# Linear attention in front of a hardswish MLP: softmax sums of five batches in 32-row column tiles, their reciprocals spread by DMA through DRAM

**Chip, cores, metric.** One core of one Trainium2 chip. The time is device microseconds of one execution of the whole program; medians of repeated runs. A difference of 2% (10.2 us here) counts as faster or slower.

## The reference, cut to what matters

```python
k_proj = einsum('ks,bhsd->bhkd', E, k)          # 8 batches, 8 heads, 1024 tokens, 64 wide -> 64 keys
v_proj = einsum('ks,bhsd->bhkd', F, v)
attn = exp(q @ k_proj.T / 8 - max)
attn = attn / (attn.sum(-1) + 1e-9)             # the softmax sums
x = (attn @ v_proj), heads side by side         # 8192 x 512
h = x @ w_in                                    # 512 -> 2048
out = (h * clip(h + 3, 0, 6) / 6) @ w_out       # 2048 -> 512
```

## The kernel before

The MLP of batch b runs as 32 "w_in groups" (4 matmuls of 128x128x512 each) and 8 "w_out groups" (16 such matmuls). The attention of batch b+1 is slipped between them at four places ("visits", n = 0 to 3, one for each w_out group). PSUM is two pools of four buffers of 128x512: `mm` and `at`.

```python
def quads(self, stationary, j, allocs):           # j: a pair of heads
    tiles = [alloc() for alloc in allocs]
    for t in range(NB):                           # two halves of the tokens
        for a in range(2):                        # two heads
            r, c = t * KP, a * D
            nc.tensor.matmul(tiles[t][c:c + D]..., stationary(r, 2 * j + a),
                             self.aT[j][r:r + KP, :, a, :], start=True, stop=True)

def sums(self, j, *allocs):                       # 64x64 tiles: each sum is made 64 times, one row for each of the 64 rows it divides
    return self.quads(lambda r, h: ones[r:r + KP, :D], j, allocs)

def visit(self, n, following, later):
    ...
    if n == 1:
        den, av = self.sums(0, pmm, pmm), self.values(0, pat, pat)
        last = self.scores(3, pat)
        recs = self.inverses(den)                 # ScalarE: Ln, then Exp(-x), 512 columns each
        self.exps(3, last)
        return lambda: self.scaled(0, av, recs)   # VectorE: values times reciprocal
    ...                                           # n = 2 and 3 alike, for j = 1, 2, 3; n = 3 also projects the next batch's k and v
```

Because the sums come out 64-fold, they stand in the rows in which the values stand, and VectorE can multiply the two tiles directly. The price is TensorE: 16 matmuls a batch for 16 distinct rows of numbers.

The softmax here doesn't subtract the row's maximum and nothing guards it: scores larger than these inputs give would overflow.

## Time and profile before

| | before |
|---|---|
| median of 6 runs | 509.23 us (509.08 to 509.76) |
| span of the profiled run | 507.8 us |
| TensorE busy | 500.3 us, 99% |
| ScalarE / VectorE busy | 274.0 / 258.2 us |
| distance of two batches, steady part | 60.62 us |

Busy time over span says who bounds. At 99% of TensorE, an instruction of another engine matters only if TensorE waits for it. The lines are shown in the prediction.

### The profile page before, as it was taken

To read this page: it belongs to the slowest core of one execution; us is meant where nothing else is said; L and a number is where in the kernel's file an instruction comes from. 1 tells how busy PE (TensorE), PEld (TensorE's weight loads), DVE (VectorE), ACT (ScalarE), POOL (GpSimd) and SP (SyncE) were. 2 spreads that over 40 slices of the span, in tenths; PEclk is the share of its full clock that TensorE was granted. 3 is DMA by queue.
4 is the path that set the end of the run, shared out by engine and by line. 5 is a ranking of instruction groups with operands and counts; after the bars stand their busy time and mean duration, and the time that the engine had idled before them with its cause. 6 is when DMAs were issued, how large, how long until landed. Compare 5 with 4: busy or idle time off the path is not lost.

```text
span 507.8 us, 7202 instructions
## 1 busy us (share of the span) xinstructions
PE 500.3 (99%) x2819; PEld 226.0 (45%) x2819; DVE 258.2 (51%) x401; ACT 274.0 (54%) x493; POOL 38.0 (7%) x57
## 2 busy tenths in 40 slices
PE   7999999999999999999999999999999999999997
PEld 3444444444444444444444444444444444444444
DVE  3572736855755733565444743467444563334420
ACT  2656476567576545664466644674447654444431
POOL 8610020010010200002000020000000000000000
PEclk9999999999999999999999999999999999999999
DMA  9999999599299593516923189411110011101112
GB/s 170 200 205 207 199 154 239 100 159 172 95 174 197 96 219 72 125 42 94 224 68 84 52 139 182 104 54 32 43 41 27 36 43 42 43 21 43 41 43 83
DMA packets 74210, 55.39 MB, mean 109 GB/s; under 512 B 35520, under 2 KB 65984, under 8 KB 74176
## 3 DMA queue, kind: packets, MB, share of 16 engines
q0 software_dynamic: 31952, 29.36, 37.1%
q1 hardware_dynamic: 42000, 25.17, 19.2%
q8 instruction: 22, 0.36, 0.3%
q10 hardware_dynamic: 224, 0.39, 0.3%
q14 instruction: 12, 0.10, 0.1%
HBM read 59.24 MB, written 16.78 MB: 150 GB/s over the span
## 4 chain that ended last, share of the span: by engine, by line
PE 96%; DMA 1%; POOL 1%; ACT 0%; issue 0%; DVE 0%; ACTq 0%; POOLq 0%
PE mm L429 44%; PE mm L462 43%; PE at L181 3%; PE mm L227 2%; DMA k<-in_k_dram 1%; PE at L227 1%; PE at L209 1%; PE mm L454 1%; PE at L349 0%; PE mm L209 0%; PE at L317 0%; POOL q L97 0%; PE at L329 0%; PE mm L349 0%; POOL k L101 0%
## 5 line engine op out<-in xcount | busy, mean ns | idle before, releaser
L435 DVE SCALAR_TENSOR_TENSOR g<-r,mm 128x512 bf16<-128x512 f32 x256 | 174.2, 687 | 135.1 <-ACT r L434 133.6
L462 PE MATMUL mm<-w_out_sb,g 128*128 128x512 bf16 x1008 | 230.9, 379 | 0.0
L429 PE MATMUL mm<-xT,w_in_sb 128*128 128x512 bf16 x1024 | 230.7, 379 | 0.0
L434 ACT ACTIVATE r<-mm 128x512 f32<-128x512 f32 x256 | 152.7, 599 | 77.2 <-PE mm L429 74.4
L429 PEld LDWEIGHTS <-w_in_sb 128*128 128x128 bf16 x1024 | 99.5, 98 | 122.1 <-issue 3.8
L462 PEld LDWEIGHTS <-g 128*128 128x128 bf16 x1008 | 96.6, 98 | 119.7 <-issue 7.0
L467 ACT COPY o_sb<-mm 128x512 f32<-128x512 f32 x35 | 20.3, 587 | 91.5 <-PE mm L462 91.5
L467 DVE COPY o_sb<-mm 128x512 f32<-128x512 f32 x28 | 19.4, 692 | 67.2 <-PE mm L462 67.2
L159 ACT ACTIVATE rec<-mm 128x512 f32<-128x512 f32 x39 | 21.7, 595 | 35.7 <-PE mm L227 20.1
L163 ACT ACTIVATE rec<-rec 128x512 f32<-128x512 f32 x60 | 35.6, 638 | 0.0
L246 DVE TENSOR_TENSOR xT<-at,rec 128x512 bf16<-128x512 f32 x42 | 26.9, 683 | 4.9 <-ACT rec L163 4.3
L218 ACT ACTIVATE aT<-at 128x512 bf16<-128x512 f32 x42 | 22.1, 617 | 0.0
L199 POOL COPY mark<-kT 1x1 bf16<-1x1 bf16 x5 | 0.9, 177 | 209.1 <-DMA kT<-kp 209.1
L159 ACT ACTIVATE rec<-at 128x512 f32<-128x512 f32 x25 | 14.7, 599 | 2.3 <-PE at L349 2.3
L181 PE MATMUL at<-k,e_t 128*64 128x512 bf16 x56 | 13.4, 382 | 0.0
L181 PE MATMUL at<-v,f_t 128*64 128x512 bf16 x56 | 13.4, 382 | 0.0
L218 ACT ACTIVATE aT<-mm 128x512 bf16<-128x512 f32 x14 | 7.6, 594 | 9.5 <-PE mm L209 9.5
L190 DVE CAST vp<-at 64x512 bf16<-64x512 f32 x14 | 9.7, 694 | 0.4
L187 DVE CAST kp<-at 64x512 bf16<-64x512 f32 x14 | 8.9, 674 | 1.1 <-PE at L181 1.1
L246 DVE TENSOR_TENSOR xT<-mm,rec 128x512 bf16<-128x512 f32 x14 | 9.0, 682 | 0.8 <-PE mm L227 0.8
L181 PEld LDWEIGHTS <-e_t 128*64 128x64 bf16 x56 | 5.6, 109 | 7.2 <-PE mm L227 2.1
L227 PE MATMUL mm<-aT,ones 64*64 64x512 bf16 x70 | 8.6, 400 | 0.0
(64 smaller groups left out, 147.0 us busy)
## 6 DMA issues: line engine op xcount, KB each, us to landing
out_dram<-o_sb SPq DMA_DIRECT2D x63, 256.0 KB, 2.0
k<-in_k_dram POOLq DMA_DIRECT2D x7, 1024.0 KB, 15.8
v<-in_v_dram POOLq DMA_DIRECT2D x7, 1024.0 KB, 20.7
q<-in_q_dram POOLq DMA_DIRECT2D x7, 1024.0 KB, 10.8
w_out_sb<-in_moe_w_out_dram POOLq DMA_DIRECT2D x4, 512.0 KB, 17.1
k<-in_k_dram POOLq DMA_DIRECT2D x4, 256.0 KB, 6.5
v<-in_v_dram POOLq DMA_DIRECT2D x4, 256.0 KB, 8.2
w_in_sb<-in_moe_w_in_dram POOLq DMA_DIRECT2D x2, 512.0 KB, 10.9
```

The lines of the kernel that those rows point to most:

```text
L159: nc.scalar.activation(ln, den, AF.Ln)
L163: nc.scalar.activation(ln, ln, AF.Exp, scale=-1.0)
L181: nc.tensor.matmul(ps[e * KP:(e + 1) * KP], ef_t[e][:, so, :], kqv[self.b]["kv"[e]][:, :, so, :], start=(so == 0), stop=(so == SO - 1))
L190: nc.vector.tensor_copy(self.vp[a * KP:(a + 1) * KP], self.ps[KP:].rearrange("p (h d) -> p h d", d=D))
L218: nc.scalar.activation(self.aT[j][:, r].rearrange("p a n -> p (a n)"), tiles[r], AF.Exp, scale=scale)
L227: nc.tensor.matmul(tiles[t][c:c + D].rearrange("p (r n) -> p r n", r=2), stationary(r, 2 * j + a), self.aT[j][r:r + KP, :, a, :], start=Tr ...
L246: nc.vector.tensor_mul(self.xT[:, j, t, :], av[t], recs[t])
L429: nc.tensor.matmul(h_ps, w_in_sb[:, ko, fo * P:(fo + 1) * P], xT[:, ko, t, :], start=(ko == 0), stop=(ko == KO - 1))
L434: nc.scalar.activation(r, h_ps, AF.Relu, bias=0.5, scale=1.0 / 6.0)
L435: nc.vector.scalar_tensor_tensor(g[:, fo, :], r, 1.0, h_ps, op0=ALU.min, op1=ALU.mult)
L462: nc.tensor.matmul(o_ps, g[:, fo, c * P:(c + 1) * P], w_out_sb[:, fo, :], start=(fo == 0), stop=(fo == FO - 1))
L467: (copy or nc.scalar.copy)(o_sb, o_ps)
```

## The change

Its intent: make each softmax sum 16 times and not 64 times, with four heads beside each other in four column tiles of 32 rows (16 rows for each half of the tokens). Since the sums then stand in other rows than the values, one of 16 rows of each goes to DRAM after Ln and Exp, and comes back broadcast over 64 rows. As that takes time, the first products (VectorE) come three w_out groups after the sums. Batches 0 to 2 keep the old way. The diff is cut to what matters: an `@@` line names each part, and `...` stands for lines or pieces left out.

```diff
+    halves = consts.tile([P, NB, KP // 4], bf16, name="halves")     # ones for the half of the rows that column t sums
...
+        def all_sums(self, alloc):
+            tiles = [alloc() for _ in range(2)]
+            for h in range(H):
+                j, a, c = h // 2, h % 2, h % 4
+                nc.tensor.matmul(tiles[h // 4][32 * c:32 * c + 32].rearrange("p (r n) -> p r n", r=2),
+                                 halves.rearrange("p t i -> p (t i)"), self.aT[j][:, :, a, :],
+                                 start=True, stop=True)
...
+        def spread(self, den):
+            few = att.tile([P, 2, TOK], f32, tag="few", name="few", bufs=1)
+            inverse(few, den)
+            rows = dram.tile([H, NB, TOK], f32, tag="rows", name="rows")
+            nc.sync.dma_start(out=rows.rearrange("(k c) t n -> (c t) k n", k=2), in_=few[::16])
+            self.recs = [rec_tile() for _ in range(KO)]
+            for h in range(H):
+                nc.sync.dma_start(out=self.recs[h // 2][h % 2 * D:(h % 2 + 1) * D]...,
+                                  in_=rows[h:h + 1]....to_broadcast([D, NB * TOK]))
...
@@ inverse: one Exp over both reciprocals (1024 columns), everywhere
+        for i, d in enumerate(den):
+            log(rec, i, d)
+        nc.scalar.activation(flat, flat, AF.Exp, scale=-1.0)
@@ visits of batches 3 to 7, by w_out group n = 0 .. 7 of the batch before
+                if (b, n) == (2, 0):
+                    return lambda: second.some_scores((2, 0, 1), six), nothing
+                if (b, n) == (2, 1):
+                    return lambda: second.some_scores((3,), six[1:2]), nothing
+                if (b, n) == (2, 3):
+                    return nothing, lambda: third.projected(pmm)
+                if n == 0:
+                    return nothing, lambda: second.some_scores(
+                        (1, 2, 3), ((pmm, pmm), (pat, pat), (pat, pmm)), third)
+                if n == 2:
+                    return second.sums_and_values, nothing
+                if n == 5:
+                    return second.first_products, nothing
+                if n == 6:
+                    return lambda: second.last_values(third), nothing
@@ output copies: on ScalarE from batch 2 on
-                rows = second_group(*behind[0], fo // SB, nc.vector.tensor_copy)
+                rows = second_group(*behind[0], fo // SB, nc.vector.tensor_copy if b == 1 else None)
@@ loads: q transposed right behind the keys; batch 4 in the order k, v, q
-                load_kqv(self.b + 1, "qkv" if self.b > 1 else "kvq")
+                load_kqv(self.b + 1, "kvq" if self.b in (1, 3) else "qkv")
```

Some buffers are shared to make room (E and F in a `g` buffer, batch 0's transposed queries in `rec` buffers). "Inside" below means in the middle of a w_out group, "after" at its end: of each pair in the code the first stands inside, the second after.

More of the change, by code (lines that the diff above doesn't have):

```diff
@@ L52 @@
     consts = ctx.enter_context(tc.tile_pool(name="consts", bufs=1))
+    dram = ctx.enter_context(tc.tile_pool(name="dram", bufs=2, space=bass.MemoryType.DRAM))
     kqv_pool = ctx.enter_context(tc.tile_pool(name="kqv", bufs=2))
@@ L69, in pat, with g_tile @@
         return ps_at.tile([P, TOK], f32, tag="at", name="at")
-    ef_f32 = consts.tile([P, S], f32, name="ef_f32")
+    def g_tile():
+        return gpool.tile([P, FO, TOK], bf16, tag="g", name="g")
+    scratch = g_tile().rearrange("p f n -> p (f n)")
+    ef_f32 = scratch[:, :2 * S].bitcast(f32)
     nc.sync.dma_start(out=ef_f32[:KP], in_=E)
@@ L77 @@
     nc.vector.memset(ones, 1.0)
+    halves = consts.tile([P, NB, KP // 4], bf16, name="halves")
+    nc.vector.memset(halves, 0.0)
+    for t in range(NB):
+        nc.vector.memset(halves[t * KP:(t + 1) * KP, t, :], 1.0)
     ident = consts.tile([P, P], bf16, name="ident")
@@ L133 @@
     f_t = consts.tile([P, SO, 2, KP], bf16, name="f_t")
-    ef_raw = consts.tile([P, S], bf16, name="ef_raw")
+    ef_raw = scratch[:, 2 * S:3 * S]
     nc.vector.tensor_copy(ef_raw[:, :S // 2], ef_f32[:, :S // 2])
@@ L155, with rec_tile, log, inverse @@
     qT_dma = {}
-    def log(den):
-        ln = att.tile([P, TOK], f32, tag="rec", name="rec", bufs=4)
-        nc.scalar.activation(ln, den, AF.Ln)
-        return ln
-    def inverse(ln):
-        nc.scalar.activation(ln, ln, AF.Exp, scale=-1.0)
-        return ln
+    def rec_tile():
+        return att.tile([P, 2, TOK], f32, tag="rec", name="rec", bufs=4)
+    def log(rec, i, den):
+        nc.scalar.activation(rec[:, i], den, AF.Ln)
+    def inverse(rec, den=()):
+        for i, d in enumerate(den):
+            log(rec, i, d)
+        flat = rec.rearrange("p i n -> p (i n)")
+        nc.scalar.activation(flat, flat, AF.Exp, scale=-1.0)
+    later = []
     class Attention:
@@ L174, in __init__, with project @@
             self.aT = {}
-        def project(self):
-            ps = self.ps = pat()
+        def project(self, alloc):
+            ps = self.ps = alloc()
             for so in range(SO):
@@ L194, in turn, with scores @@
             nc.sync.dma_start_transpose(self.kT, self.kp.rearrange("p h a d -> p (h a d)"))
-            if self.b == 1:
-                qT_dma[1] = q_transposed(1)
+            last = self.kT[:1, 0, :1]
+            if self.b not in (2, 3):
+                qT_dma[self.b] = q_transposed(self.b)
+                last = qT_dma[self.b][:1, 0, 0, :1]
             if self.b + 1 < B:
                 mark = att.tile([1, 1], bf16, tag="mark", name="mark")
-                nc.gpsimd.tensor_copy(mark, self.kT[:1, 0, :1] if self.b > 1 else qT_dma[1][:1, 0, 0, :1])
-                load_kqv(self.b + 1, "qkv" if self.b > 1 else "kvq")
-        def scores(self, j, alloc):
+                nc.gpsimd.tensor_copy(mark, last)
+                load_kqv(self.b + 1, "kvq" if self.b in (1, 3) else "qkv")
+        def scores(self, j, *allocs):
             qT = qT_dma[self.b]
-            tiles = [alloc() for _ in range(2)]
+            tiles = [alloc() for alloc in allocs]
             for a in range(2):
@@ L236, in values, with scaled @@
             return self.quads(lambda r, h: self.vp[r:r + KP, h, :], j, allocs)
-        def inverses(self, den):
-            recs = [log(d) for d in den]
-            for rec in recs:
-                inverse(rec)
-            return recs
-        def scaled(self, j, av, recs):
-            for t in range(NB):
-                nc.vector.tensor_mul(self.xT[:, j, t, :], av[t], recs[t])
-        def visit(self, n, following, later):
+        def scaled(self, j, av, rec):
+            for t in range(NB):
+                nc.vector.tensor_mul(self.xT[:, j, t, :], av[t], rec[:, t])
@@ new lines, in all_sums @@
+        def all_sums(self, alloc):
[5 more added lines that the diff above has]
+                                 start=True, stop=True)
+            return tiles
+        def spread(self, den):
[5 more added lines that the diff above has]
+            for h in range(H):
+                nc.sync.dma_start(out=self.recs[h // 2][h % 2 * D:(h % 2 + 1) * D].rearrange("d t n -> d (t n)"),
+                                  in_=rows[h:h + 1].rearrange("h t n -> h (t n)").to_broadcast([D, NB * TOK]))
@@ new lines, in projected, with some_scores @@
+        def projected(self, alloc=pat):
+            self.project(alloc)
+            self.keys_out()
+            rest = [lambda a=a: self.values_out(a) for a in range(2)]
+            if alloc == pmm:
+                for r in rest:
+                    r()
+                rest = []
+            later.extend([self.turn] + rest)
+        def some_scores(self, js, allocs, following=None):
+            tiles = [self.scores(j, *alloc) for j, alloc in zip(js, allocs)]
+            for j, two in zip(js, tiles):
+                self.exps(j, two)
+            if following:
+                following.projected()
@@ new lines, in sums_and_values, with first_products, last_values @@
+        def sums_and_values(self):
+            den = self.all_sums(pmm)
+            self.av = [self.values(j, pat, pat) for j in range(2)]
+            self.spread(den)
+        def first_products(self):
+            for j in range(2):
+                self.scaled(j, self.av[j], self.recs[j])
+        def last_values(self, following):
+            av = [self.values(2, pmm, pmm), self.values(3, pat, pat)]
+            if following:
+                following.some_scores((0,), ((pat, pat),))
+            for i in range(2):
+                self.scaled(2 + i, av[i], self.recs[2 + i])
@@ L252, in visit @@
+        def visit(self, n, following):
             if n == 0:
-                last = self.scores(2, pmm)
-                firsts = [self.scores(j, pat) for j in range(2)]
-                for j, tiles in zip((2, 0, 1), (last, *firsts)):
-                    self.exps(j, tiles)
+                self.some_scores((2, 0, 1), ((pmm, pmm), (pat, pat), (pat, pat)))
                 return lambda: None
@@ L259, in visit @@
                 den, av = self.sums(0, pmm, pmm), self.values(0, pat, pat)
-                last = self.scores(3, pat)
-                recs = self.inverses(den)
+                last = self.scores(3, pat, pat)
+                rec = rec_tile()
+                inverse(rec, den)
                 self.exps(3, last)
-                return lambda: self.scaled(0, av, recs)
+                return lambda: self.scaled(0, av, rec)
             if n == 2:
@@ L266, in visit @@
                 more = self.sums(2, pat, pat)
-                recs = self.inverses(den)
-                self.recs = []
-                later += [lambda i=i: self.recs.append(log(more[i])) for i in range(NB)]
-                later += [lambda i=i: inverse(self.recs[i]) for i in range(NB)]
-                return lambda: self.scaled(1, av, recs)
+                rec, self.rec = rec_tile(), rec_tile()
+                inverse(rec, den)
+                later.extend([lambda i=i: log(self.rec, i, more[i]) for i in range(NB)])
+                later.append(lambda: inverse(self.rec))
+                return lambda: self.scaled(1, av, rec)
             den = self.sums(3, pmm, pat)
@@ L274, in visit @@
             av = self.values(3, pat, pat)
-            recs = self.inverses(den)
-            self.scaled(2, early, self.recs)
+            rec = rec_tile()
+            inverse(rec, den)
+            self.scaled(2, early, self.rec)
             if following:
-                following.project()
-                later += [following.turn] + [lambda a=a: following.values_out(a) for a in range(2)]
+                following.project(pat)
+                later.extend([following.turn] + [lambda a=a: following.values_out(a) for a in range(2)])
             def rest():
-                self.scaled(3, av, recs)
+                self.scaled(3, av, rec)
                 if following:
@@ L331, in queries @@
                                             ident)
-            q = att.tile([P, 2 * TOK], bf16, tag="qTp", name="qTp", bufs=3)
+            q = rec_tile().rearrange("p i n -> p (i n)").bitcast(bf16)[:, :2 * TOK]
             nc.vector.tensor_copy(q[:, :len(js) * TOK], ps)
@@ L372, in sums @@
             def sums(j):
-                ln = log(self.sums(0, j, pmm))
                 recs[j] = opool.tile([P, TOK], f32, tag="o_sb", name="o_sb")
-                nc.scalar.activation(recs[j], ln, AF.Exp, scale=-1.0)
+                nc.scalar.activation(recs[j], self.sums(0, j, pmm), AF.Ln)
+                nc.scalar.activation(recs[j], recs[j], AF.Exp, scale=-1.0)
             def products(j):
@@ L421, in second_values @@
             av = [self.values(1, i, pat) for i in js]
-            lns = [log(d) for d in den]
-            for i, a, ln in zip(js, av, lns):
-                nc.vector.tensor_mul(self.xT[:, i, 1, :], a, inverse(ln))
+            rec = rec_tile()
+            inverse(rec, den)
+            for i, (j, a) in enumerate(zip(js, av)):
+                nc.vector.tensor_mul(self.xT[:, j, 1, :], a, rec[:, i])
     def h_part(h_ps, xT, t, fo, kos):
@@ L475, in x_tile @@
         return xpool.tile([P, KO, NB, TOK], bf16, tag="xT", name="xT")
-    def g_tile():
-        return gpool.tile([P, FO, TOK], bf16, tag="g", name="g")
     xT = x_tile()
@@ L500 @@
             first.queries(1, (0, 1) if fo == FO - 2 else (2, 3))
-    behind, later = [], []
+    behind = []
     second = Attention(1)
@@ L521 @@
         if fo == 7:
-            second.project()
-            second.keys_out()
-            later += [second.turn, *(lambda a=a: second.values_out(a) for a in range(2))]
+            second.projected()
         elif fo == 11:
@@ L531 @@
             if i == 0:
-                rest.append(second.visit(c, None, later))
+                rest.append(second.visit(c, None))
             elif i == 2 or c == SB - 1:
@@ L545, with visits, nothing @@
         third = Attention(b + 2) if b + 2 < B else None
-        n = 0
+        def visits(b, n):
+            def nothing():
+                pass
+            if b == 1:
+                n -= SB
+                if n < 3:
+                    return lambda: second.visit(n, third), nothing
+                return nothing, lambda: second.visit(n, third)()
+            if b + 1 < B:
+                six = (pmm, pmm), (pat, pat), (pat, pat)
+                if (b, n) == (2, 0):
[13 more added lines that the diff above has]
+                    return lambda: second.last_values(third), nothing
+            return nothing, nothing
         for t in range(NB):
@@ L558 @@
                 pop()
-                if b > 1 and t == 0 and fo == 5 and third:
-                    qT_dma[b + 2] = q_transposed(b + 2)
                 if b == 1 and t == 0 and fo == 10:
-                    second.project()
-                    second.keys_out()
-                    later += [second.turn, *(lambda a=a: second.values_out(a) for a in range(2))]
+                    second.projected()
                 if not behind or fo % SB < SB - 1:
                     continue
-                if b + 1 == B or n == 4:
-                    whole(second_group(*behind[0], fo // SB))
-                    continue
-                rows = second_group(*behind[0], fo // SB, nc.vector.tensor_copy)
-                if n < 3:
-                    next(rows)
-                    next(rows)
-                    rest = second.visit(n, third, later)
-                    whole(rows)
-                else:
-                    whole(rows)
-                    rest = second.visit(n, third, later)
-                rest()
-                n += 1
+                inside, after = visits(b, t * SB + fo // SB)
+                rows = second_group(*behind[0], fo // SB, nc.vector.tensor_copy if b == 1 else None)
+                next(rows)
+                next(rows)
+                rest = inside()
+                whole(rows)
+                after()
+                if rest:
+                    rest()
             behind = [(b, t, g)]
```

## The prediction

> **What bounds the kernel now.** I read the page first: the busy time of the engines and the chain that ended last.
>
> ```profile
> PE 500.3 (99%) x2819; PEld 226.0 (45%) x2819; DVE 258.2 (51%) x401; ACT 274.0 (54%) x493; POOL 38.0 (7%) x57
> ...
> PE 96%; DMA 1%; POOL 1%; ACT 0%; issue 0%; DVE 0%; ACTq 0%; POOLq 0%
> PE mm L429 44%; PE mm L462 43%; PE at L181 3%; PE mm L227 2%; DMA k<-in_k_dram 1%; PE at L227 1%; PE at L209 1%; PE mm L454 1%; PE at L349 0%; PE mm L209 0%; PE at L317 0%; POOL q L97 0%; PE at L329 0%; PE mm L349 0%; POOL k L101 0%
> ```
>
> TensorE sets the time: 99% busy, 96% of the chain. VectorE and ScalarE are half idle, so relieving them is worth nothing by itself. Only two things count: TensorE passes taken out, and waits of TensorE put in. Next the timeline of TensorE over one whole attention batch in the steady part (batch 7, worked on beside the w_out groups of batch 6). Columns: start, length, instruction, count.
>
> ```profile
> 379.50 1.89 PE L462 MATMUL mm<-w_out_sb,g 128*128 128x512 bf16 x8
> 381.32 0.41 PE L209 MATMUL mm<-qT,kT 64*64 64x256 bf16 x8
> 381.56 0.61 PE L209 MATMUL at<-qT,kT 64*64 64x256 bf16 x16
> 382.10 1.90 PE L462 MATMUL mm<-w_out_sb,g 128*128 128x512 bf16 x8
> 383.84 3.62 PE L429 MATMUL mm<-xT,w_in_sb 128*128 128x512 bf16 x16
> 387.29 1.89 PE L462 MATMUL mm<-w_out_sb,g 128*128 128x512 bf16 x8
> 389.11 0.41 PE L227 MATMUL mm<-aT,ones 64*64 64x512 bf16 x4
> 389.35 0.39 PE L227 MATMUL at<-aT,vp 64*64 64x512 bf16 x4
> 389.57 0.39 PE L209 MATMUL at<-qT,kT 64*64 64x256 bf16 x8
> 389.89 1.90 PE L462 MATMUL mm<-w_out_sb,g 128*128 128x512 bf16 x8
> ```
>
> There is no gap in it. A group of 16 large matmuls takes 3.453 us (383.84 to 387.29), 0.2158 us each. Four 64x64 matmuls of 512 columns (sums at 389.11, values at 389.35, scores at 389.57) advance the clock by 0.21 to 0.24 us together: they run side by side as one **pass** of 0.213 us. The block of three passes costs 389.89 - 387.29 - 8 x 0.2158 = 0.87 us, of which 3 x 0.213 = 0.64 is work; the other 0.23 is two **switches** of tile shape, 0.115 us each. The same blocks recur every 60.62 us (258.26, 318.88, 379.50).
>
> The third view is the timeline of ScalarE at the first attention block of batch 3, where six exponentials follow one another, and that of VectorE beside it:
>
> ```profile
> 139.15 1.09 ACT L218 ACTIVATE aT<-mm 128x512 bf16<-128x512 f32 x2 [1.48 <-PE mm L209]
> 140.12 2.08 ACT L218 ACTIVATE aT<-at 128x512 bf16<-128x512 f32 x4
> 142.41 0.60 ACT L434 ACTIVATE r<-mm 128x512 f32<-128x512 f32 x1 [0.22 <-PE mm L429]
> ...
> 141.55 0.69 DVE L467 COPY o_sb<-mm 128x512 f32<-128x512 f32 x1 [1.61 <-PE mm L462]
> ```
>
> Here the reader is to see that ScalarE is taken from 139.15 to 142.20 (0.49 us from start to start), and that the w_out result of that moment is copied out by VectorE at 141.55, so it does not queue behind the exponentials. The fourth is the load of a batch, from GpSimd's timeline and the list of DMA issues of 290 to 350 us (columns of the second: KB each, us to landing):
>
> ```profile
> 292.53 0.18 POOL L199 COPY mark<-kT 1x1 bf16<-1x1 bf16 x1 [57.14 <-DMA kT<-kp]
> 293.04 0.88 POOL L115 DMA_DIRECT2D q<-in_q_dram  x1 [0.34 <-issue]
> ...
> v<-in_v_dram POOLq DMA_DIRECT2D x1, 1024.0 KB, 21.4
> kT<-kp SPq DMA_TRANSPOSE x1, 2.6
> qT<-q SPq DMA_TRANSPOSE x1, 6.8
> ```
>
> From the mark to v landed is about 2.2 + 21.4 = 23.6 us.
>
> **What the Trainium skill says.** "TensorEngine Tiling (Array Packing)", Key Properties: tiles work independently, and a change of tiling mode drains the array. The trace agrees with both: four 64x64 matmuls in one pass, 0.115 us a switch. "TensorE: Matmul & The Clock Gate", Measured speedup vs the span model: three column tiles of M=32 gave 2.38 times; four aren't listed. The trace has only two column tiles beside each other (the projection, 128x64: 16 matmuls in 8 steps of 0.215 us); it has no 128x32. "DMA: Bandwidth & Descriptors", Two DMAs through the same engine are not ordered: a DMA that reads what another wrote must wait for its semaphore. So the spread through DRAM is two trips in series. The trace can't show that yet; a 256 KB output lands after 2.0 us.
>
> **Part by part.** The sums of batches 1 and 2 stay as they are.
>
> *Passes.* Sums were 4 passes a batch (16 matmuls, 64x64). They become 8 matmuls of 128x32, four column tiles beside each other, so 2 passes, if four really run together. Saved: 5 batches x 2 x 0.213 = 2.13 us.
>
> *Switches.* Before, a steady batch had four blocks with 2 switches each and one more into the projection: 9. After, a steady batch (4, 5, 6) has scores and projection at n=0 (3), sums and values at n=2 (3: two shapes), values and the next batch's first scores at n=6 (2): 8. Batch 3, spread over five places: 11 against 9. Batch 7, without a projection behind it: 7 against 8. Net -2, or -0.23 us. The batch-7 place before (values of n=3) has a further 0.08 us wait (406.87 + 0.21 + 0.10 = 407.18, next matmul at 407.26), which goes. Sum of what is **removed: 2.4 us**.
>
> *ScalarE.* 16 Ln and Exp of about 0.49 us a batch become 2 Ln and one Exp of 1024 columns. About 5 us less a batch, beside TensorE: worth 0. VectorE loses the output copies of these batches (0.69 us each) to ScalarE: that matters only where ScalarE is taken.
>
> *New waits on PSUM.* The four mm buffers go round. (a) Batch 3, n=0: the w_out copy is now on ScalarE, in order behind six exponentials. It would start at 142.20 and end about 142.8; the second w_in group takes that buffer and is due at 141.35 + 0.86 = 142.21. Wait: about **0.65 us**. (b) Batch 7, n=0: the three scores come after the whole w_out group and take three mm buffers. With Te the end of that group: copy at Te+0.2, exponentials Te+0.7 to Te+3.75; the fourth w_in group, due at Te+3.45, needs the buffer of the last: 0.35 us. The next w_out group then needs the first relu and product, which come behind the exponentials: ready Te+5.05, due Te+4.66: 0.4 us. Together **0.75 us**. Batches 4 to 6 have the projection (1.73 us) between, which covers this. (c) Batch 3, n=3: the projection sits in an mm buffer until four VectorE copies (2.5 us) are through; the fourth w_in group is due at the same moment: 0.1 us. Sum **added: 1.5 us**.
>
> *The spread.* 32 KB out (some 2 us), then eight loads of 256 KB, 2 MB. At the 215 GB/s that the loads reach here it is an estimate of 10 us, so 15 us from the sums; the first products come three w_out groups later, 3 x 6.9 = 20.7 us, and need only the first half. Hidden, even if a load beside it slows it: a q transpose beside a load took 14 us against 5 on the queue, and half of a doubled spread still fits.
>
> *Batch 5's load.* The tightest place. Batch 4's keys are projected near 164 us, its kT goes out at about 167.2; kT and qT in a row took 8.6 us for batch 1 (58.25 to 66.84), so the mark falls at 176 and v lands at about 199.5. The projection of batch 5, now at n=0, is due near 202: 2.5 us to spare, of which the tail of the spread can take 1 or 2. Expected loss 0.3 us.
>
> Sum: -2.4 + 1.5 + 0.3 = -0.6 us, so **508.6 us**.
>
> **Rivals.** *Four column tiles don't run together.* Then the sums take 4 passes as before, the 2.13 us fall away, and the time is about 510.8. For it: nothing with 128x32 is in the trace. Against it: two column tiles do run beside each other, and the skill's 2.38 of 3. I give it 15%. *Batch 5's load, or the spread, is late.* If the eight loads hold up kT and qT by 5 us, TensorE waits some 3 us once: 511.5. If the spread took over 20 us in every batch, VectorE would stand in order before the products, and all five batches would lose microseconds: 515 to 525. The first has 15%, the second 4%. *The PSUM waits don't come* (another buffer order than I assume): then the full 2.4 us show, 506.8; 20%. *ScalarE relieved speeds the kernel up by per cents*: the profile speaks against it, TensorE has no wait to give back.
>
> **Range and chances.** 2% is 10.2 us. The whole of what is removed is 2.4 us, so faster by over 2% is as good as excluded (0.01). Slower by over 2% needs a repeated DMA wait of 2 us or more in each batch (0.03). The rest is within 2%. The range runs from the full saving without waits (506.6) to a late load or serial column tiles (511.2).
>
> **What would show it.** Right: 40 sums matmuls of 128x32 with starts in fours, two steps of 0.21 us; the distance of two batches' blocks down from 60.62 to about 60.1 us; TensorE waits of 0.3 to 0.7 us at batch 3's and batch 7's first blocks, put down to ScalarE's copy or exponentials; ScalarE's busy time down by some 25 us or more; no wait for k or v at batch 5's projection. Wrong: eight sums in four steps or more, a wait of TensorE for a DMA, or VectorE products that wait for the spread.

## The result

| | before | after |
|---|---|---|
| median of 6 runs | 509.23 us | 508.28 us (507.85 to 508.47) |
| ratio | | 0.9978, 95% interval 0.9966 to 0.9991 |
| span of the profiled run | 507.8 us | 506.4 us |
| TensorE busy, matmuls | 500.3 us, 2819 | 499.8 us, 2779 |
| ScalarE busy | 274.0 us | 256.2 us |
| VectorE busy | 258.2 us | 246.2 us |
| moved by DMA | 55.39 MB | 66.02 MB |

Ratios are the mean time of one kernel's fast runs over that of the other's fast runs of the same rounds, so not quite the ratio of the medians. "Same" at 2%, but the interval does not reach 1: the change gains 0.2%.

From the page of the kernel after, engines and chain:

```profile
PE 499.8 (99%) x2779; PEld 225.3 (44%) x2779; DVE 246.2 (49%) x384; ACT 256.2 (51%) x438; POOL 37.9 (7%) x57
...
PE 96%; ACT 2%; DVE 1%; issue 0%; ACTq 0%
```

ScalarE lost 18 us and VectorE 12 us of work, and the time fell by 1: TensorE bounds as before. Now TensorE's timeline after, around the sums of batch 6, with all three places of a steady batch (the lines of the projection, 1.72 us long, are left out):

```profile
318.52 3.62 PE L528 MATMUL mm<-w_out_sb,g 128*128 128x512 bf16 x16
322.07 0.41 PE L226 MATMUL mm<-qT,kT 64*64 64x256 bf16 x8
...
335.07 1.89 PE L528 MATMUL mm<-w_out_sb,g 128*128 128x512 bf16 x8
336.89 0.62 PE L264 MATMUL mm<-aT,halves 128*32 128x512 bf16 x8
337.44 0.63 PE L244 MATMUL at<-aT,vp 64*64 64x512 bf16 x8
337.99 1.90 PE L528 MATMUL mm<-w_out_sb,g 128*128 128x512 bf16 x8
...
363.90 1.89 PE L528 MATMUL mm<-w_out_sb,g 128*128 128x512 bf16 x8
365.73 0.41 PE L244 MATMUL mm<-aT,vp 64*64 64x512 bf16 x4
...
382.14 0.41 PE L226 MATMUL mm<-qT,kT 64*64 64x256 bf16 x8
```

Eight sums matmuls take 337.44 - 336.89 = 0.55 us: two passes of 0.216 and the switch to the next shape. The same block of the next batch stands 382.14 - 322.07 = 60.07 us later (60.62 before).

**Where the time went.** The w_in groups are the same 256 in both kernels, so the start of each is a mile post. From TensorE's timelines, in us:

| stretch (first w_in group to first w_in group) | before | after | difference |
|---|---|---|---|
| start to batch 0 | 20.89 | 20.70 | -0.19 |
| batch 0, first half | 27.07 | 27.59 | +0.52 |
| to batch 2 | 85.45 | 85.48 | +0.03 |
| batch 2's MLP (attention of batch 3) | 60.77 | 61.15 | +0.38 |
| batches 3, 4, 5 (attention of 4, 5, 6), each | 60.62 | 60.07 | -0.55 |
| batch 6 (attention of 7) | 58.83 | 58.67 | -0.16 |
| batch 7, to the last w_out matmul | 69.00 | 69.00 | 0.00 |
| last matmul to the end | 3.94 | 3.56 | -0.38 |

They add up to -1.45 us. The first line is start-up: in the runs below, whose code up to there is the same as after's, it lies anywhere from 20.45 to 21.29. The last line I can't explain: the issues and landings there are alike in both traces, and of the kernel before there is one trace. It scatters, too: 3.54 to 3.62 us in eleven of the experiments below, 4.95 in e8. That leaves -0.88 us between the first w_in group and the last w_out matmul.

Batch 2's line holds more than waits. It has two passes less (-0.43), but also one pass more (+0.22), since batch 4's first scores moved into it, two switches more (+0.23), and 0.33 and 0.06 us of waits. In batch 6's line that one pass is missing, with two passes and a switch less, and a wait of 0.67 us hides most of it.

Three waits of TensorE that the kernel before doesn't have stand in the trace after. The one in batch 0, the kernel before first:

```profile
45.04 0.39 PE L349 MATMUL at<-aT,vp 64*64 64x512 bf16 x4
...
44.61 0.41 PE L414 MATMUL at<-aT,ones 64*64 64x512 bf16 x4
44.85 0.91 PE L414 MATMUL at<-aT,vp 64*64 64x512 bf16 x4
45.69 2.76 PE L528 MATMUL mm<-w_out_sb,g 128*128 128x512 bf16 x12
```

Before, four such values matmuls took 0.39 us; here 0.91. The `at` buffers of the pair of heads before are freed by VectorE's products, and those start at 44.01 against 43.62 us before, because the single Exp of 1024 columns ends later than the first of two. The second, at batch 4's projection (n = 3 of batch 2), and the third, at batch 7's scores:

```profile
166.09 3.94 PE L495 MATMUL mm<-xT,w_in_sb 128*128 128x512 bf16 x16
169.87 3.62 PE L528 MATMUL mm<-w_out_sb,g 128*128 128x512 bf16 x16
...
382.93 3.94 PE L495 MATMUL mm<-xT,w_in_sb 128*128 128x512 bf16 x16
387.05 3.61 PE L528 MATMUL mm<-w_out_sb,g 128*128 128x512 bf16 x16 [0.19 <-DVE g L501]
```

An undisturbed run of 16 large matmuls (a w_out group, or four w_in groups) lasts 3.453 us from start to start. The first here lasts 169.87 - 166.09 = 3.78, so 0.33 us are lost; the second 387.05 - 382.93 = 4.12, so 0.67 us.

And one wait that I had predicted is not there, the w_out copy of batch 3's first place, now on ScalarE behind six exponentials (ScalarE's timeline, then TensorE's):

```profile
140.48 2.08 ACT L235 ACTIVATE aT<-at 128x512 bf16<-128x512 f32 x4
142.39 0.65 ACT L533 COPY o_sb<-mm 128x512 f32<-128x512 f32 x1
```

```profile
141.77 3.62 PE L495 MATMUL mm<-xT,w_in_sb 128*128 128x512 bf16 x16
145.23 1.89 PE L528 MATMUL mm<-w_out_sb,g 128*128 128x512 bf16 x8
```

The copy ends at 143.04, as late as I had worked out, but the w_in groups beside it run through (141.77 to 145.23 is 3.46).

### The profile page after: what moved, and what is told of

The parts are those of the page before. It is cut to its first block, busy times and chain, and to the rows that moved or that the text cites. A ratio compares the mean times of both kernels' runs of the same rounds, so it can differ in the third digit from the quotient of the medians.

```text
span 506.4 us, 7084 instructions
## 1 busy us (share of the span) xinstructions
PE 499.8 (99%) x2779; PEld 225.3 (44%) x2779; DVE 246.2 (49%) x384; ACT 256.2 (51%) x438; POOL 37.9 (7%) x57
## 2 busy tenths in 40 slices
DMA packets 77529, 66.02 MB, mean 130 GB/s; under 512 B 36200, under 2 KB 66664, under 8 KB 77496
## 4 chain that ended last, share of the span: by engine, by line
PE 96%; ACT 2%; DVE 1%; issue 0%; ACTq 0%
PE mm L528 43%; PE mm L495 43%; PE at L195 2%; PE mm L93 1%; PE at L244 1%; PE at L226 1%; PE mm L244 1%; PE mm L520 1%; PE mm L264 1%; ACT aT L235 0%; PE at L382 0%; PE at L414 0%; PE mm L226 0%; PE at L394 0%; PE mm L195 0%; PE at L366 0%
## 5 line engine op out<-in xcount | busy, mean ns | idle before, releaser
L533 ACT COPY o_sb<-mm 128x512 f32<-128x512 f32 x55 | 32.1, 586 | 124.0 <-PE mm L528 124.0
L235 ACT ACTIVATE aT<-at 128x512 bf16<-128x512 f32 x38 | 20.2, 615 | 9.1 <-PE at L226 9.1
L235 ACT ACTIVATE aT<-mm 128x512 bf16<-128x512 f32 x18 | 10.3, 613 | 3.6 <-PE mm L226 3.6
L533 DVE COPY o_sb<-mm 128x512 f32<-128x512 f32 x8 | 5.5, 687 | 13.4 <-PE mm L528 13.4
L195 PE MATMUL at<-v,f_t 128*64 128x512 bf16 x48 | 11.5, 382 | 0.0
L195 PE MATMUL at<-k,e_t 128*64 128x512 bf16 x48 | 11.5, 382 | 0.0
L176 ACT ACTIVATE rec<-rec 128x1024 f32<-128x1024 f32 x10 | 10.6, 1061 | 0.3
L170 ACT ACTIVATE rec<-mm 128x512 f32<-128x512 f32 x10 | 5.5, 595 | 7.9 <-PE mm L244 5.4
L93 PE MATMUL mm<-ones 128*128 128x512 bf16 x19 | 7.8, 539 | 1.5 <-DVE halves L84 1.5
L170 ACT ACTIVATE few<-mm 128x512 f32<-128x512 f32 x10 | 5.4, 594 | 7.4 <-PE mm L264 7.4
```

The costliest lines, as they stand in the source:

```text
L93: nc.tensor.matmul(ps, ones[:, :P], ones, start=True, stop=True)
L170: nc.scalar.activation(rec[:, i], den, AF.Ln)
L176: nc.scalar.activation(flat, flat, AF.Exp, scale=-1.0)
L195: nc.tensor.matmul(ps[e * KP:(e + 1) * KP], ef_t[e][:, so, :], kqv[self.b]["kv"[e]][:, :, so, :], start=(so == 0), stop=(so == SO - 1))
L235: nc.scalar.activation(self.aT[j][:, r].rearrange("p a n -> p (a n)"), tiles[r], AF.Exp, scale=scale)
L533: (copy or nc.scalar.copy)(o_sb, o_ps)
```

## The experiments

All are edits of the kernel after (the diffs are shortened with `...`), and all gave the right result. Of some I use the time, of most the trace: most effects are 0.3 to 2 us and single runs of one kernel differ by up to 2.2 us, while a stretch of TensorE's timeline is the same to 0.02 us from run to run. The medians of the kernel before in the three sessions were 509.61, 509.65 and 509.48 us.

**e1: the sums twice.**

```diff
-            for h in range(H):
+            for h in 2 * list(range(H)):
```

> The changed kernel with each of the eight 128x32 sums matmuls issued twice, h0..h7 and again h0..h7, so 4 passes a batch as before the change. Theory A (the gain is TensorE passes removed, each four column tiles side by side): 2 passes x 0.213 us x 5 batches = +2.1 us over the changed kernel, 510.4 us, and the sums block in the trace 0.43 us longer. Rival (the gain comes from ScalarE relieved or from fewer blocks, and the sums hide beside something): 508.3 us, no change.

Measured: 510.42 us, ratio to before 1.0017 (1.0003 to 1.0031). In the trace the stretch with the sums is 0.44 us longer in the first of the batches and 0.43 in each of the others, +2.16 in all. With as many passes as before the change, its gain is gone. ScalarE's relief and the longer schedule are as in the kernel after, so they are not what gains.

**e2: the same eight in another order.**

```diff
-            for h in range(H):
+            for h in (0, 4, 1, 5, 2, 6, 3, 7):
```

> The changed kernel with the same eight sums matmuls in another order (0,4,1,5,2,6,3,7), so that neighbours share a column tile. Theory A (a matmul runs beside its neighbour only if that is in another column tile, and starts are in order): five steps in place of two, 3 x 0.213 x 5 = +3.2 us, 511.5 us. Rival (the four tiles aren't what saves: the eight matmuls would be that fast in any order, for example because the 32 columns are cheap): 508.3 us.

Measured: ratio 0.9977 (0.9962 to 0.9993), as the kernel after. TensorE's timeline:

```profile
154.63 0.62 PE L264 MATMUL mm<-aT,halves 128*32 128x512 bf16 x8
155.19 0.41 PE L244 MATMUL at<-aT,vp 64*64 64x512 bf16 x4
```

0.56 us, against 0.55. My theory A fell in the part about the order: a matmul that waits for its column tile doesn't hold back the next one in another tile. It left open whether four tiles beside each other are the saving at all, or whether 32 columns are cheap in themselves. So e9.

**e9: eight more, all in one column tile.**

```diff
             tiles = [alloc() for _ in range(2)]
+            for h in range(H):
+                nc.tensor.matmul(tiles[0][:32].rearrange("p (r n) -> p r n", r=2),
+                                 halves.rearrange("p t i -> p (t i)"), self.aT[h // 2][:, :, h % 2, :],
+                                 start=True, stop=True)
```

> The changed kernel with eight more sums matmuls of 128x32 in each of batches 3 to 7, all into the same 32 rows of one PSUM tile, ahead of the right ones (which overwrite them; the result stays right). e1 added eight over four column tiles: 0.43 us a batch. Theory A (each column tile works through its own matmuls, and what is saved is running four tiles beside each other): 8 steps x 0.216 = 1.73 us a batch, 8.6 us in all, 516.9 us. Rival (a 32-column matmul is cheap in itself, whichever column tile): 0.43 us a batch as in e1, 510.4 us.

Measured: 517.02 us, ratio 1.0153 (1.0138 to 1.0169); in the trace +1.72 us in each of the five batches. Eight matmuls over four column tiles cost 0.43 us (e1), the same eight in one tile 1.72, eight passes of 0.215. TensorE's timeline, with the eight extra at L263 and the right ones at L268:

```profile
154.73 1.47 PE L263 MATMUL mm<-aT,halves 128*32 128x512 bf16 x6
155.83 0.40 PE L268 MATMUL mm<-aT,halves 128*32 128x512 bf16 x3
156.04 0.38 PE L263 MATMUL mm<-aT,halves 128*32 128x512 bf16 x1
156.05 0.39 PE L268 MATMUL mm<-aT,halves 128*32 128x512 bf16 x3
156.25 0.38 PE L263 MATMUL mm<-aT,halves 128*32 128x512 bf16 x1
156.47 0.59 PE L268 MATMUL mm<-aT,halves 128*32 128x512 bf16 x2
```

Six of the right sums start (155.83 and 156.05) while the extra ones, issued before them, are still being worked off. Only two come last, 0.216 us apart. By the program these are heads 0 and 4, the only ones of the eight in the column tile of the extra ones; they write two different PSUM tiles, so it is not the writing of the same PSUM tile that holds them apart. That settles it: the saving is the four tiles beside each other, and each tile works off its own matmuls in turn.

**e3: two exponentials at the start again.**

```diff
-            inverse(rec, den)
+            for i, d in enumerate(den):
+                log(rec, i, d)
+            for i in range(2):
+                nc.scalar.activation(rec[:, i], rec[:, i], AF.Exp, scale=-1.0)
```

> The changed kernel, but in the second half of batch 0 the two reciprocals are two exponentials of 512 columns again, not one of 1024. Theory A (the 0.5 us that TensorE loses at 45 us of the changed kernel is a wait for an at buffer that VectorE frees later, because the first product now waits for both reciprocals): -0.5 us against the changed kernel, 507.8 us, and the four values matmuls near 45 us back at 0.39 us together. Rival (start-up jitter of the loads): no change of that spot, 508.3 us.

Measured: the stretch of batch 0 is 0.52 us shorter, and the four values matmuls are back:

```profile
45.06 0.41 PE L414 MATMUL at<-aT,ones 64*64 64x512 bf16 x4
45.30 0.39 PE L414 MATMUL at<-aT,vp 64*64 64x512 bf16 x4
45.62 2.76 PE L531 MATMUL mm<-w_out_sb,g 128*128 128x512 bf16 x12
```

Theory A holds. The time (508.24 us, ratio 0.9982) does not resolve it: the profiled run's start-up alone came 0.45 us later than after's. The effect is read from the trace alone.

**e4: batch 3's copy back on VectorE.**

```diff
-                ... nc.vector.tensor_copy if b == 1 else None)
+                ... nc.vector.tensor_copy if b == 1 or (b, t, fo) == (2, 0, SB - 1) else None)
```

> The changed kernel, with the one w_out copy at batch 3's first block back on VectorE. My prediction's step (a) said that this copy on ScalarE costs TensorE 0.65 us: then the w_in group after that block starts 0.65 us earlier, relative to its neighbours. Rival, read since from the trace of the changed kernel (no wait there; the mm buffers come back in the order in which the program releases them, so the copied buffer goes to the fourth w_in group, not the second): the stretch from that block to the next w_in group but one is the same within 0.05 us, and the time is 508.3 us within noise.

One look (profiled run 509.83 us, state unknown). From the group before that block to the next w_in group but one, each stretch is within 0.01 us of the kernel after. The copy was never waited for, on either engine; the rival holds.

**e5: batch 7's scores inside the w_out group.**

```diff
+                if n == 0 and third is None:
+                    return lambda: second.some_scores((1, 2, 3), six), nothing
```

> The changed kernel, but batch 7's three scores stand in the middle of the w_out group (as batch 3's do) and take two mm and four at buffers. Theory A (step (b) of the prediction: TensorE waits 0.67 us there for the last exponential's mm buffer and for the relu behind six exponentials): -0.6 to -0.7 us, 507.6 us, and no wait in the w_in group after it. Rival (the wait only moves into the middle of the group, as ScalarE has the same six exponentials and a copy to do): -0.2 us or less.

Measured: that stretch is 0.66 us shorter; 508.03 us, ratio 0.9971 (0.9959 to 0.9984). Theory A. Half a w_out group (1.73 us) between the scores and the next w_in group covers the exponentials, as the projection does in the other batches.

**e6: batch 4's copies shared by two engines.**

```diff
-            self.keys_out()                       # 2 copies, and 2 of the values, all on VectorE
+            for a, copy in enumerate((nc.vector.tensor_copy, nc.scalar.copy)): ...   # keys
+            for a, copy in enumerate((nc.vector.tensor_copy, nc.scalar.copy)): ...   # values
```

> The changed kernel, but the four copies out of batch 4's projection are split between VectorE and ScalarE. Theory A (step (c): the fourth w_in group waits for the mm buffer of the projection until VectorE has done four copies, 0.32 us in the trace): -0.3 us, 508.0 us, the group back at 3.45 us. Rival (it waits for the products of the w_in groups behind the copies, or ScalarE's relu is delayed as much): the group stays over 3.6 us.

Measured: 0.39 us worse at that place (508.86 us, which alone would not resolve it). The rival holds, in its second reason: ScalarE's relu is delayed. VectorE's timeline, then ScalarE's and TensorE's:

```profile
166.56 0.68 DVE L287 CAST kp<-mm 64x512 bf16<-64x512 f32 x1 [4.02 <-PE mm L195]
167.89 0.69 DVE L289 CAST vp<-mm 64x512 bf16<-64x512 f32 x1 [0.65 <-ACT kp L287]
```

```profile
167.28 0.58 ACT L287 CAST kp<-mm 64x512 bf16<-64x512 f32 x1 [2.01 <-DVE kp L287]
168.62 0.58 ACT L289 CAST vp<-mm 64x512 bf16<-64x512 f32 x1 [0.76 <-DVE vp L289]
169.22 2.06 ACT L503 ACTIVATE r<-mm 128x512 f32<-128x512 f32 x4
```

```profile
170.59 3.61 PE L531 MATMUL mm<-w_out_sb,g 128*128 128x512 bf16 x16 [0.32 <-DVE g L504]
```

ScalarE's first relu waits behind its copies until 169.22 (167.17 in the kernel after), and the w_out group then waits for VectorE's product of it. The copies gained nothing in return, as the engines take turns. The program makes them: each copy out of the one PSUM tile carries a wait for the other engine's copy before it. For two copies of the same rows the Trainium skill, "PSUM — Partial Sum Buffer", PSUM bank collisions raise a hardware error, says why: two engines must not touch the same bank and 32-partition quadrant at once, reads against reads included. I had not looked there. The trace agrees as far as it can: no two of the four overlap. The wait in the middle, of the values (rows 64 to 127) for the keys (rows 0 to 63), is not of that kind; the program has it all the same, and no run here tries it without.

**e7: the first products one w_out group earlier.**

```diff
-                if n == 5:
+                if n == 4:
                     return second.first_products, nothing
```

> The changed kernel with the first products two w_out groups after the sums and not three. Theory A (the spread lands near 19 us after the sums in batches 4 and 5, beside a load of keys and values, and 10 us after them in the others; VectorE then stands in order before the products and TensorE runs out of mm buffers): 1 to 2.5 us lost in each of batches 4 and 5, none in the others, +2 to +5 us, 510.5 to 513 us. Rival (as my prediction had it, the first half of the spread is there some 12 us after the sums, even beside a load): no change, 508.3 us.

Measured: 510.75 us, ratio 1.0028 (1.0012 to 1.0044). In the trace batches 4 and 5 lose 1.71 and 1.87 us, the others nothing. VectorE's timeline, then TensorE's, in batch 4:

```profile
232.87 1.29 DVE L257 TENSOR_TENSOR xT<-at,rec 128x512 bf16<-128x512 f32 x2 [0.91 <-DMA rec<-rows]
237.13 1.29 DVE L257 TENSOR_TENSOR xT<-at,rec 128x512 bf16<-128x512 f32 x2 [2.97 <-DMA rec<-rows]
238.34 2.47 DVE L501 SCALAR_TENSOR_TENSOR g<-r,mm 128x512 bf16<-128x512 f32 x4
```

```profile
239.06 3.61 PE L528 MATMUL mm<-w_out_sb,g 128*128 128x512 bf16 x16 [1.55 <-DVE g L501]
```

VectorE stands before the products until 237.13 and only then makes the g tiles that TensorE needs. In the kernel after the products start at 238.28: the third group is needed, and its margin in batch 4 is little more than 1 us (237.13 to 238.28, two runs). Theory A holds. The profiled run was the slowest of four (512.28; the others 510.05 to 511.00), so the trace shows more than the median loss; why the runs differ isn't shown.

**e12: batch 4 loaded q first.**

```diff
-                load_kqv(self.b + 1, "kvq" if self.b in (1, 3) else "qkv")
+                load_kqv(self.b + 1, "kvq" if self.b == 1 else "qkv")
```

> The changed kernel with batch 4 loaded in the order q, k, v again. Theory A (this part of the change is worth nothing here: v would land near 161.5 us, before its projection at 164.2, because the transposition of q no longer runs beside this load): no wait of TensorE at that projection, 508.3 us within noise. Rival (k and v first is what keeps TensorE from waiting there): a wait of 1 us or more at batch 4's projection, put down to the DMA of v.

One look (508.77 us, state unknown): no stretch from batch 0 on differs from the kernel after by more than 0.01 us. Theory A: this part alone is worth nothing here.

**e8, e10, e11: the mends together.** e8 is e3, e5 and e6; e10 is e3 and e5; e11 is e10 with all four copies of batch 4's projection on ScalarE.

> Edits of e3, e5 and e6 together. Theory A (the three waits are separate and TensorE takes the whole gain): -0.52 -0.67 -0.32 = -1.5 us, 506.8 us. Rival (a wait removed comes back further on): less than half of it, over 507.5 us.

> Edits of e3 and e5 together, without e6's, which made batch 4's wait longer. Theory (the two waits are separate): -0.52 - 0.67 = -1.2 us against the changed kernel, 507.1 us; by the trace, from the first w_in group of batch 0 to the last w_out matmul, 1.2 us less. Rival: a wait comes back elsewhere, less than 0.6 us.

> As e10, and all four copies out of batch 4's projection on ScalarE (0.49 us from start to start against VectorE's 0.61). Theory (what matters is when the last of the four copies ends; in e6 two engines took turns and lost 0.2 us at each change): the buffer is free 0.5 us earlier, -0.2 to -0.3 us more than e10, 506.9 us. Rival (ScalarE's relu then comes 1 us later and TensorE waits for that): no gain over e10 or up to 0.2 us loss.

| | median | ratio to before | from batch 0's first w_in group to the last w_out matmul, against after |
|---|---|---|---|
| after | 508.28 us | 0.9978 | |
| e8 | 507.72 us | 0.9969 (0.9956 to 0.9983) | -0.79 us |
| e10 | 507.49 us | 0.9958 (0.9946 to 0.9971) | -0.89 us |
| e11 | 506.96 us | 0.9951 (0.9938 to 0.9965) | -1.16 us |

e8 falls short of the expected -1.5 by what e6 had shown (+0.39 where I had counted -0.32). e10 takes -0.52 and -0.66, and gives 0.28 back at batch 1's projection, where TensorE reaches v before it has landed (e10's timeline of TensorE):

```profile
54.52 0.40 PE L195 MATMUL at<-k,e_t 128*64 128x512 bf16 x1
54.83 0.38 PE L195 MATMUL at<-v,f_t 128*64 128x512 bf16 x1
```

In every other projection that I looked at, the two start within 0.01 us. The wait belongs to this execution: v landed at 54.79 us in it, but at 53.86 in e8 and 53.77 in e11, which have e3's edit too and no such wait. e11's place does not gain by the trace: the four w_in groups after the projection run through, but the w_out group behind them then waits for VectorE's products (165.46 to 169.25 is 3.79 us, against 3.78 with the copies on VectorE). The wait only moved, as the rival said, so the traces of e11 and e10 differ by that one wait for v, and e11's own edit is not shown to gain. (Its expectation put a change of engine at 0.2 us; by e6's lines, 166.56 to 167.28 us is 0.72 against VectorE's own 0.61, so 0.1.) By the intervals both are faster than the kernel before (all within the 2% that count as the same). Against the kernel after (0.9966 to 0.9991) e10's interval overlaps and e11's just doesn't, and they ran in different sessions; of their edits, e3's and e5's are shown to gain by the traces.

## Why the prediction was right, point by point

The time, 508.28 us, lies 0.3 us from the 508.6 predicted, which is less than start-up alone scatters by (20.45 to 21.29). By its own steps:

- **Passes, -2.13 us: right.** Two passes for eight sums matmuls; e1 takes it back with +2.16, e9 shows that the column tiles are the cause. Rival 1 (15%, serial tiles) is out.
- **Switches, -0.23 us, and the small wait before batch 7: right as far as the traces resolve it.** Batches 4 to 6 gain 0.55 us each, the predicted 2 x 0.213 + 0.115 = 0.54.
- **ScalarE's relief, worth 0: right.** 18 us less of ScalarE with a gain that e1 cancels by passes alone. My "25 us or more" was too high: I had not set the output copies that come to ScalarE against it (55 in place of 35, 0.59 us each).
- **(a) 0.65 us at batch 3's first place: wrong, it is 0.** The failed step is "the second w_in group takes that buffer". e4 shows that the copy isn't waited for. Why, I read from the waits in the trace before: there the second and third w_in group of that place wait for ScalarE, the fourth for VectorE. So the buffers come back in the order in which the program releases them, and the exponentials stand before the copy; the copied buffer goes to the fourth group, due 1.7 us later. That order is read from the traces, not tried by itself.
- **(b) 0.75 us at batch 7: right**, 0.67 in its two parts: 0.32 for the fourth w_in group (0.35 predicted) and 0.35 for the w_out group (0.4). e5 removes it.
- **(c) 0.1 us at batch 4's projection: the place right, the size short**, 0.33. The fourth w_in group starts late by that much. I had put the four copies at 2.5 us; in the trace they last from 166.23 to 168.94, 2.7 us, and the group was due at 166.09 + 3 x 0.863 = 168.68.
- **The spread, hidden: right, but my time for it was short.** I worked out 15 us for all of it. From the sums to the last landing that the trace has, it is 15.9 us in batch 6 (336.89 to 352.81), but 21.2 beside a load in batch 4 (216.74 to 237.92): there the rows' trip to DRAM lasts 5.4 us and not 2, and a 256 KB return lands after 8.6 us (see below). e7 shows that two groups would not have been enough.
- **Batch 5's load: no wait.** v was issued at 179.72 and landed about 20.5 us later, near 200.2; the projection stands at 202.70. The 2.5 us to spare are as predicted, and the 0.3 us that I had allowed for it were not used.
- **Not seen at all: +0.52 us in batch 0**, from the one part of the diff that I passed over as worth 0, the joint Exp. I had worked out only that it doesn't hold up the w_in groups, not that VectorE's later products free the `at` buffers later (e3).

So the mechanism of the gain held, while the good agreement of the number is in part luck: (a) was too much by 0.65 and batch 5's load by 0.3, batch 0 too little by 0.52 and (c) by 0.23, and these largely cancel.

## What to carry to other kernels

When one engine is at 99%, count its passes and its waits, and put down the relief of the others as nothing. A wait for a buffer is worked out only when you know which buffer comes next: find the order of release in the trace before (which engine the next users wait for) before you price a copy that moves. And an instruction merged into a longer one ends later for its first reader, so look who waits for that reader, two steps on.

## What the Trainium skill lacked or had wrong

- "TensorE: Matmul & The Clock Gate", The mechanism: it says that matmuls keep program order in start and end, with no reordering. e2 speaks against it for column tiles: with neighbours in the same tile, in order starts would need five passes (1.08 us); the block took 0.56 us with its switch, as in the other order. e9's timeline shows it directly: matmuls in other column tiles start at 155.83, two earlier issued ones at 156.04 and 156.25.
- The same page, Measured speedup vs the span model, has three column tiles (2.38 times) but not four: eight 128x32 matmuls of 512 columns took 0.43 us over four tiles (e1) and 1.72 us in one (e9), 4.0 times.
- The same page, LDWEIGHTS, gives columns / 1.2 ns, so by estimate 27 ns for 32 columns and 107 for 128; the profile shows 94 ns for 128x32 and 98 ns for 128x128. Whether these lengths are the load alone no run here tests; in the kernel after the loads overlapped the matmuls.
- "TensorEngine Tiling (Array Packing)", Key Properties, says that a change of mode drains the array but not what it costs: 0.115 us here.
- "DMA: Bandwidth & Descriptors" has no figure for a write to DRAM that is read back beside a running load. From the issue of the 32 KB write to that of the first read: 3.6, 5.4 and 5.5 us beside a load, 2.0 us twice without. From the timeline of the DMA queue after, with a load and without:

```profile
219.39 0.64 SPq L274 DMA_DIRECT2D rows<-few  x1
224.75 5.22 SPq L277 DMA_DIRECT2D rec<-rows  x8
...
339.54 0.64 SPq L274 DMA_DIRECT2D rows<-few  x1
341.51 4.94 SPq L277 DMA_DIRECT2D rec<-rows  x8
```

Of the eight broadcast reads of 256 KB in each block the trace has four landings: after 8.6 us (median) beside the load and 6.4 us without; issuing them took some 0.62 us each.
